# Reordering the fill, the block transitions and the last product of a scan-then-MLP kernel

## The chip, the cores and the metric

The kernel runs on one core of a Trainium2 chip. PE (TensorE) does the matrix products, ACT (ScalarE) and DVE (VectorE) the elementwise work, and SP (SyncE) and POOL (GpSimd) mainly issue DMA transfers. The metric is device time in microseconds (us); a lower one is better. Every time below is a median of the runs of one kernel, with lowest and highest.

## The reference

```python
# batch 4, seq 6144, d_model 256, d_ff 1024
sig = 1/(1 + exp(-f_logit));  f = lb + (1 - lb)*sig;  i = 1 - f
h[t] = f[t]*h[t-1] + i[t]*x[t]          # over the sequence, y[t] = h[t]
out = maximum(y @ w1, y @ w2) @ w_out   # on the 24576 x 256 rows of y
```

## The kernel before

Tokens are handled in 48 blocks of 512. For each block ACT makes the sigmoid ("gate"), DVE makes decay, drive and two scans (one for each half of the channels), PE does the "first layer" (8 groups `fc` of two 512-column matmuls, evicted in pairs by an ACT ReLU), and then the second layer. Blocks 0 to 3 use a plain second layer: 8 pieces of five 256-column matmuls. From block 4 on, two blocks make a pair, and their second layer is a scheme with seven products instead of eight. The input comes in chunks: one block each for the first four, then one pair each, so chunk 4 is blocks 4 and 5. `fT` and `xT` are the transposed `f_logit` and `x` of a chunk, `wd` is the first layer's weight. The instruction order on each engine is the order of the program (`manual_schedule`), so the text below is also the schedule. Lines that the change and the argument touch, with cuts marked:

```python
    nc.vector.tensor_copy(out=ident[:], in_=ident_f[:])
    nc.scalar.activation(out=warm[:], in_=ident_f[:, 0:1], func=AF.Sigmoid)
    nc.vector.tensor_scalar_add(out=nom[:], in0=lbc[:], scalar1=-1.0)   # need lower_bound
    nc.vector.tensor_scalar(out=om[:], in0=lbc[:], scalar1=-1.0, scalar2=1.0, ...)
    fetch_first(0); fetch_first(1)            # ... f_logit and x of block 0, in halves
    ...
    first_bf16(0, 0, nc.vector.tensor_copy)   # casts of the first half
    first_bf16(0, 1, nc.vector.tensor_copy)
    first_turn(0); first_recurrence(0)
    ...
    for fc in range(FC):                      # second layer of block 0
        if fc == 4:
            turn(turn_steps(2)); gate(2)
        second_layer(0, fc)
    ...
    for fc in range(FC):                      # first layer of block 1, alone
        first_layer(1, fc)
    ...
    order = {2: ("decay0", "drive0"), 3: ("scan00",), 4: ("scan01",), ...}   # block 4's, in
    for fc in range(FC):                                                     # block 3's layer
        first_layer(3, fc); second_layer(2, fc)
        if fc in gates: pair_gate(PAIR0, gates[fc])     # gates = {0: 0, 1: 1, 4: 2, 5: 3}
        for t in order.get(fc, ()): scans[PAIR0][t]()
    ...
            for slot in range(2 * FC):        # pair loop
                first_layer(2 * p + slot // FC, slot % FC)
                if first and slot % 2:        # first pair: second layer of block 3
                    second_layer(2 * p - 1, slot // 2)
    # last pair, last product (M4): bank X already holds the sum for another output
    product("X", part(1, 1), given(t4), groups=range(3));           then(leave_last(slice(0, 3)))
    product("Y", part(1, 1), given(t4), True, groups=range(3, 4));  then(leave_last(slice(3, 4)))
```

A group in the fresh bank Y needs what bank X held added later, so ACT takes a snapshot of that group of X before M4 starts. DVE reads bank X first.

Of the kernel before, what the change touches and what calls it, by code (L numbers as in the profile page):

```python
# [18 lines left out]
def kernel(  # L19
# [105 lines left out]
    def first_bf16(k, s, copy):  # L125
        raw = raws[k, s]
        nat = const.tile([P, TB // 2 // P, D], HALF, name=f"nat{k}{s}")
        copy(out=nat[:], in_=raw[:])
        raws[k, s] = nat
# [48 lines left out]
    def turn(steps):  # L178
        for dst, src in steps:
            nc.tensor.transpose(dst, src, ident[:])  # L180
# [276 lines left out]
    def store(j, osb, groups=slice(0, TB // P), cols=slice(0, D), queue=None):  # L457
        b, t0, nb, c, o = blocks[j]
        r0 = b * S + t0
        (queue or nc.sync).dma_start(  # L460
            out=out[r0 : r0 + nb, :].rearrange("(p n) d -> p n d", p=P)[
                :, groups, cols
            ],
            in_=osb[:, groups, cols],
        )
# [58 lines left out]
    def sevenths(p):  # L524

        bank, snap, osbs = {}, {}, {}
        steps = []
        ja, jb = 2 * p, 2 * p + 1
        end = p == NPAIR - 1

        def product(b, left, w, fresh=False, groups=range(TB // P)):
            for i in groups:
                for k in range(KH + 1):
                    new = fresh and i == groups[0] and k == 0
                    steps.append([b, left, w(k), i, k, new, None])

        def then(fn):
            steps[-1][-1] = fn

        def open_bank(b, i=0):  # L540
            if i:
                t = ps_d.tile([P, 2 * TB // P, P], FP32, name="dT")
            else:
                t = ps_o.tile([P, TB // P, P], FP32, name="ps")
            bank[b] = t

        def seed(b, src):
            def go():
                open_bank(b)
                nc.scalar.copy(out=bank[b][:], in_=bank[src][:])  # L550
            return go

        def snapshot(b, name):
            def go():
                t = snpool.tile([P, TB // P, P], FP32, name="sn")
                nc.scalar.copy(out=t[:], in_=bank[b][:])  # L556
                snap[name] = t
            return go

        def leave(b, j, cols, name, last):  # L560
            def go():
                if j not in osbs:
                    osbs[j] = opool.tile([P, TB // P, D], FP32, name="osb")
                dst = osbs[j][:, :, cols]
                if name is None:
                    nc.scalar.copy(out=dst, in_=bank[b][:])  # L566
                else:
                    nc.vector.tensor_tensor(  # L568
                        out=dst, in0=bank[b][:], in1=snap[name][:], op=ALU.add
                    )  # L570
                if end:
                    store(j, osbs[j], cols=cols)
                elif last:
                    store(j, osbs[j])
            return go

        def leave_both(b):
            def go():
                leave(b, jb, hi, 5, False)()
                t = snpool.tile([P, TB // P, P], FP32, name="sn")  # L580
                nc.scalar.copy(out=t[:, 3, :], in_=bank[b][:, 3, :])
                snap[4] = t
            return go

        def leave_last(at):
            def go():
                dst = osbs[jb][:, at, lo]
                if at.start:
                    nc.vector.tensor_tensor(
                        out=dst, in0=bank["Y"][:, at, :], in1=snap[4][:, at, :],  # L590
                        op=ALU.add,
                    )
                else:
                    nc.scalar.copy(out=dst, in_=bank["X"][:, at, :])
                store(jb, osbs[jb], at, lo, nc.sync if at.start else nc.scalar)
            return go

        def sub(n):
            return lambda: sums[p, n]

        def part(t, k2):
            return lambda: rts[2 * p + t, k2]

        def plain(k2, cols):
            a, b = right(k2, cols)
            return lambda k: a[:, k, :] if k < KH else b

        def given(t):
            return lambda k: t[:, k, :]

        product("X", part(0, 0), plain(0, lo), True)
        then(seed("B", "X"))
        product("E", sub(1), given(t1), True)
        then(snapshot("E", 5))
        if end:
            product("B", part(0, 1), plain(1, lo), groups=range(1))
            product("X", sub(2), given(t2))
            then(snapshot("X", 2))
            product("B", part(0, 1), plain(1, lo), groups=range(1, 4))
            then(leave("B", ja, lo, None, False))  # L620
            product("X", sub(3), given(t3))
            then(leave_both("X"))
            product("E", sub(4), plain(1, hi))
            then(leave("E", ja, hi, 2, True))
            product("X", part(1, 1), given(t4), groups=range(3))
            then(leave_last(slice(0, 3)))
            product("Y", part(1, 1), given(t4), True, groups=range(3, 4))
            then(leave_last(slice(3, 4)))
        else:
            product("X", sub(2), given(t2))  # L630
            then(snapshot("X", 2))
            product("B", part(0, 1), plain(1, lo))
            then(leave("B", ja, lo, None, False))
            product("X", sub(3), given(t3))
            then(leave("X", jb, hi, 5, False))
            product("E", sub(4), plain(1, hi))
            then(leave("E", ja, hi, 2, True))
            product("X", part(1, 1), given(t4))
            then(leave("X", jb, lo, None, True))

        def runner(step):
            b, left, w, i, k, fresh, after = step

            def run():
                if fresh:
                    open_bank(b, i)
                a = left()
                cols = slice(i * P, (i + 1) * P) if k < KH else slice(i, TB, TB // P)
                nc.tensor.matmul(  # L649
                    bank[b][:, i, :],  # L650
                    lhsT=a[:, k, cols],
                    rhs=w,
                    start=fresh,
                    stop=after is not None,
                    skip_group_check=True,
                )
                if after is not None:
                    after()
            return run

        return [runner(s) for s in steps]

    with tc.manual_schedule():
        nc.scalar.dma_start(out=lbc[:], in_=lower_bound.rearrange("(h p) -> p h", p=P))
        nc.vector.tensor_copy(out=ident[:], in_=ident_f[:])
        nc.scalar.activation(out=warm[:], in_=ident_f[:, 0:1], func=AF.Sigmoid)
        nc.vector.tensor_scalar_add(out=nom[:], in0=lbc[:], scalar1=-1.0)
        nc.vector.tensor_scalar(
            out=om[:], in0=lbc[:], scalar1=-1.0, scalar2=1.0, op0=ALU.mult, op1=ALU.add
        )  # L670
        fetch_first(0)
        fetch_first(1)
        for g in range(NG):
# [11 lines left out]
            nc.tensor.transpose(wt[:, 0, 0:P], ident[:], ident[:])  # L685
        first_bf16(0, 0, nc.vector.tensor_copy)
        first_bf16(0, 1, nc.vector.tensor_copy)
        first_turn(0)
        first_recurrence(0)
        first_bf16(1, 0, nc.scalar.copy)  # L690
# [30 lines left out]
        for fc in range(FC):  # L721
            if fc == 4:
                turn(turn_steps(2))
                gate(2)
            second_layer(0, fc)
        for step in scan_steps(2):
            step()
        for step in make_sevens():
            step()
        for fc in range(FC):  # L730
            first_layer(1, fc)
        turn(turn_steps(3))
        gate(3)
        early = scan_steps(3)
# [21 lines left out]
                scans[PAIR0][t]()  # L756

        queue, due = [], 0
        for p in range(PAIR0, NPAIR):
            first = p == PAIR0  # L760
            more = p + 1 < NPAIR
# [23 lines left out]
            gates = {4: 0, 6: 1, 12: 2, 14: 3} if more else {}  # L785
            for slot in range(2 * FC):
                first_layer(2 * p + slot // FC, slot % FC)
                if first and slot % 2:
                    second_layer(2 * p - 1, slot // 2)
                if p > PAIR0 + 1 or (p == PAIR0 + 1 and slot >= LAG):  # L790
                    due += NSEV / (2 * FC)
                    while due >= 1:
                        due -= 1
                        queue.pop(0)()
                if slot == 2 and p + 3 < NPAIR:
                    cross(blocks[2 * p + 6][3])
                if slot in gates:
                    pair_gate(p + 1, gates[slot])
                while seq and seq[0][0] < (slot + 1) * 9:
                    seq.pop(0)[1]()  # L800
# [38 lines left out]
```

## Time and profile before

380.15 us (380.11 to 380.67, three runs); the profiled execution spans 378.5 us. From the page of the kernel before, the busy line and the chain of waits:

```profile
PE 367.7 (97%) x4136; PEld 279.2 (74%) x4136; DVE 338.4 (89%) x409; ACT 302.4 (80%) x410; POOL 36.2 (10%) x79
...
PE 92%; DVE 5%; DMA 1%; ACT 0%; issue 0%; DVEq 0%
```

PE is the bound: only time in which PE cannot issue can be won. From the first weights on, the starts of successive matmuls are 216, 109 and 56 ns apart (512, 256 and 128 columns) except at a few places, and each place has an owner.

The fill. From the timeline of the kernel before (start us, busy us, engine, line, operation, tiles, in brackets the idle time before and who ended it), DVE:

```profile
4.63 0.17 DVE L667 TENSOR_SCALAR nom<-lbc 128x2 f32<-128x2 f32 x1 [3.06 <-DMA lbc<-in_lower_bound_dram]
4.71 0.16 DVE L668 TENSOR_SCALAR om<-lbc 128x2 f32<-128x2 f32 x1
4.78 0.42 DVE L128 CAST nat<-osb 128x512 f16<-128x512 f32 x1
...
6.53 0.48 DVE L213 TENSOR_SCALAR ff<-u,nom 128x256 f16<-128x256 f16 x2 [0.72 <-ACT u L258]
6.93 0.68 DVE L223 TENSOR_TENSOR v<-u,ps 128x512 f16<-128x512 f16 x1
```

The cast of f_logit waits behind two tiny operations that wait for lower_bound (complete at 4.61 us); f_logit itself is complete at 4.28 us. The decay (6.53) and the drive (6.93) follow, and the first `wd` matmul comes at 11.75 us.

Blocks 0 to 1. The timeline, PE and then ACT:

```profile
23.97 1.89 PE L441 MATMUL dT<-r,wd 128*128 128x512 f16 x8
26.11 1.94 PE L441 MATMUL dT<-r,wd 128*128 128x512 f16 x8 [0.25 <-ACT r L449]
...
25.04 1.94 ACT L449 ACTIVATE r<-dT 128x1024 f16<-128x1024 f32 x2 [0.28 <-PE dT L441]
```

With nothing between the groups, PE outruns the evictions of its two banks. By the spacing of the starts it loses 0.41 us here (the bracket's 0.25 is shorter because the end of a pipelined matmul is modelled), and 0.05 us a little later.

Into block 4. The timeline, ACT and DVE; the landing of chunk 4's f_logit after its transposing DMA, at 38.12 us, starts this chain:

```profile
38.23 0.63 ACT L285 ACTIVATE u<-fT 128x512 f16<-128x512 f16 x1 [0.95 <-DMA fT<-scr]
38.77 1.00 ACT L449 ACTIVATE r<-dT 128x1024 f16<-128x1024 f32 x1
39.67 0.62 ACT L285 ACTIVATE u<-fT 128x512 f16<-128x512 f16 x1
...
40.32 0.35 DVE L213 TENSOR_SCALAR ff<-u,nom 128x512 f16<-128x512 f16 x1 [1.07 <-ACT u L285]
40.59 0.69 DVE L223 TENSOR_TENSOR v<-u,xT 128x1024 f16<-128x1024 f16 x1
41.19 0.69 DVE L496 COPY osb<-ps 128x512 f32<-128x512 f32 x1
41.79 2.45 DVE L230 TENSOR_TENSOR_SCAN r<-ff,r,v 128x512 f16<-128x512 f16 x2
```

Gate, eviction, gate, decay, drive, copy, two scans follow each other without a gap and end at 44.25 us. Block 4's first layer began at 44.42 us; only its second matmul (44.64 us) needs the second scan. So there was no wait yet, and little room.

Into block 7. The timeline, DVE and then PE:

```profile
50.26 0.69 DVE L496 COPY osb<-ps 128x512 f32<-128x512 f32 x1 [1.81 <-PE ps L487]
...
57.00 0.69 DVE L496 COPY osb<-ps 128x512 f32<-128x512 f32 x1
57.60 1.48 DVE L506 TENSOR_TENSOR S<-r 128x2560 f16<-128x2560 f16 x1
...
60.40 2.46 DVE L230 TENSOR_TENSOR_SCAN r<-ff,r,v 128x512 f16<-128x512 f16 x2
...
58.91 0.22 PE L649 MATMUL ps<-w,r 128*128 128x128 f16 x1
59.14 0.51 PE L649 MATMUL ps<-t,S 128*128 128x128 f16 x6
...
62.23 0.38 PE L441 MATMUL dT<-r,wd 128*128 128x512 f16 x1
62.91 0.38 PE L441 MATMUL dT<-r,wd 128*128 128x512 f16 x1 [0.30 <-DVE r L230]
```

DVE sits idle 1.81 us for a copy of block 3's output and then works without pause to the scan that PE waits for; PE loses 0.46 us. On the way it loses another 0.17 us: its product at 59.14 us needs the sum `S` that DVE makes right after the second copy (57.60 to 59.08).

The end. The timeline, ACT and then PE:

```profile
372.29 0.27 ACT L581 COPY sn<-ps 128x128 f32<-128x128 f32 x1 [1.27 <-DVE osb L568]
...
372.37 0.22 PE L649 MATMUL ps<-w,S 128*128 128x128 f16 x1
372.61 1.00 PE L649 MATMUL ps<-t,r 128*128 128x128 f16 x15
```

M4 starts 0.24 us after the last matmul before it, once ACT's snapshot has left bank X.

### The profile page before, as it was taken

To read this page: it belongs to the slowest core of one execution; us is meant where nothing else is said; L and a number is where in the kernel's file an instruction comes from. 1 tells how busy PE (TensorE), PEld (TensorE's weight loads), DVE (VectorE), ACT (ScalarE), POOL (GpSimd) and SP (SyncE) were. 2 spreads that over 40 slices of the span, in tenths; PEclk is the share of its full clock that TensorE was granted. 3 is DMA by queue.
4 is the path that set the end of the run, shared out by engine and by line. 5 is a ranking of instruction groups with operands and counts; after the bars stand their busy time and mean duration, and the time that the engine had idled before them with its cause. 6 is when DMAs were issued, how large, how long until landed. Compare 5 with 4: busy or idle time off the path is not lost.

```text
span 378.5 us, 9591 instructions
## 1 busy us (share of the span) xinstructions
PE 367.7 (97%) x4136; PEld 279.2 (74%) x4136; DVE 338.4 (89%) x409; ACT 302.4 (80%) x410; POOL 36.2 (10%) x79
## 2 busy tenths in 40 slices
PE   4999999999999999999999999999999999999995
PEld 3677767777777777777777777777777777777784
DVE  4796789999999999999999999999999999999762
ACT  5856788888798798888888887987988888889752
POOL 2500203101101101101001101101101101000000
PEclk9999999999999999999999999999999999999999
DMA  7996999999999989989999999999999999940223
GB/s 248 249 225 130 285 145 222 168 187 258 221 185 264 214 175 283 186 164 266 169 236 263 220 205 301 196 197 276 209 192 270 211 174 188 236 196 4 112 113 113
DMA packets 104797, 77.17 MB, mean 204 GB/s; under 512 B 93554, under 2 KB 95602, under 8 KB 104050
## 3 DMA queue, kind: packets, MB, share of 16 engines
q1 hardware_dynamic: 101538, 51.19, 59.9%
q0 software_dynamic: 2544, 25.17, 33.8%
q8 instruction: 32, 0.52, 0.6%
q10 hardware_dynamic: 672, 0.20, 0.2%
q14 instruction: 11, 0.09, 0.1%
HBM read 53.48 MB, written 48.23 MB: 269 GB/s over the span
## 4 chain that ended last, share of the span: by engine, by line
PE 92%; DVE 5%; DMA 1%; ACT 0%; issue 0%; DVEq 0%
PE ps L649 45%; PE dT L441 42%; PE ps L487 4%; DVE r L230 1%; DVE S L506 1%; DMA lbc<-in_lower_bound_dram 1%; PE ps L180 1%; DVE v L223 1%; DVE r L264 1%; DVE ff L213 0%; PE ps L397 0%; DVE osb L496 0%; ACT r L449 0%; PE ps L137 0%; ACT u L258 0%
## 5 line engine op out<-in xcount | busy, mean ns | idle before, releaser
L449 ACT ACTIVATE r<-dT 128x1024 f16<-128x1024 f32 x192 | 196.0, 1023 | 52.6 <-PE dT L441 52.5
L441 PE MATMUL dT<-r,wd 128*128 128x512 f16 x768 | 225.3, 379 | 1.1 <-DVE wd L365 0.5
L649 PEld LDWEIGHTS <-S 128*128 128x128 f16 x1760 | 115.4, 101 | 37.8 <-issue 0.6
L649 PEld LDWEIGHTS <-r 128*128 128x128 f16 x1320 | 90.9, 101 | 36.7
L230 DVE TENSOR_TENSOR_SCAN r<-ff,r,v 128x512 f16<-128x512 f16 x88 | 108.2, 1271 | 0.8
L649 PE MATMUL ps<-t,S 128*128 128x128 f16 x1320 | 101.6, 219 | 0.0
L506 DVE TENSOR_TENSOR S<-r 128x2560 f16<-128x2560 f16 x44 | 65.4, 1487 | 14.4 <-ACT r L449 14.3
L441 PEld LDWEIGHTS <-wd 128*128 128x128 f16 x768 | 67.6, 113 | 6.4 <-DVE wd L365 1.6
L649 PE MATMUL ps<-wob,r 128*128 128x128 f16 x704 | 69.9, 219 | 0.0
L506 DVE TENSOR_TENSOR S<-r,S 128x2560 f16<-128x2560 f16 x44 | 65.0, 1478 | 0.0
L285 ACT ACTIVATE u<-fT 128x512 f16<-128x512 f16 x88 | 56.1, 637 | 0.9 <-DMA fT<-scr 0.9
L213 DVE TENSOR_SCALAR ff<-u,nom 128x512 f16<-128x512 f16 (+1 forms) x98 | 31.5, 346 | 8.3 <-ACT u L207 3.5
L649 PE MATMUL ps<-w,r 128*128 128x128 f16 x176 | 38.5, 219 | 0.0
L348 POOL CAST waited<-fT 128x1 f32<-128x1 f16 x21 | 9.4, 449 | 280.6 <-DMA fT<-scr 280.6
L649 PE MATMUL ps<-t,r 128*128 128x128 f16 x435 | 34.4, 219 | 0.0
L568 DVE TENSOR_TENSOR osb<-ps,sn 128x512 f32<-128x512 f32 x44 | 30.1, 685 | 3.2 <-PE ps L649 3.2
L649 PE MATMUL ps<-wob,S 128*128 128x128 f16 x352 | 32.6, 219 | 0.0
L223 DVE TENSOR_TENSOR v<-u,xT 128x1024 f16<-128x1024 f16 x44 | 30.2, 686 | 0.0
L556 ACT COPY sn<-ps 128x512 f32<-128x512 f32 x44 | 25.9, 588 | 2.6 <-PE ps L649 2.4
L566 ACT COPY osb<-ps 128x512 f32<-128x512 f32 x43 | 25.1, 583 | 0.8 <-PE ps L649 0.8
L487 PEld LDWEIGHTS <-r 128*128 128x128 f16 x160 | 16.0, 101 | 6.2
L649 PE MATMUL ps<-w,S 128*128 128x128 f16 x88 | 19.3, 219 | 0.0
(58 smaller groups left out, 129.9 us busy)
## 6 DMA issues: line engine op xcount, KB each, us to landing
out_dram<-osb SPq DMA_DIRECT2D x46, 512.0 KB, 4.0
scr<-in_f_logit_dram POOLq DMA_DIRECT2D x22, 512.0 KB, 7.5
scr<-in_x_dram POOLq DMA_DIRECT2D x22, 512.0 KB, 10.4
r<-in_moe_w_dram SPq DMA_DIRECT2D x4, 512.0 KB, 6.9
fT<-in_f_logit_dram POOLq DMA_DIRECT2D x3, 256.0 KB, 7.6
xT<-in_x_dram POOLq DMA_DIRECT2D x3, 256.0 KB, 8.3
out_dram<-osb SPq DMA_DIRECT2D x3, 256.0 KB, 2.6
osb<-in_f_logit_dram SPq DMA_DIRECT2D x2, 256.0 KB, 4.5
```

Of the source, the lines that this page charges most:

```text
L213: nc.vector.tensor_scalar(out=ff[:, h, cols], in0=u[:, h, cols], scalar1=nom[:, h : h + 1], scalar2=1.0, op0=ALU.mult, op1=ALU.add,)
L223: nc.vector.tensor_tensor(out=like(v[:, :, cols], xT), in0=like(u[:, :, cols], xT), in1=xT, op=ALU.mult,)
L230: nc.vector.tensor_tensor_scan(out=y_of(j, h), data0=ff[:, h, o : o + TB], data1=v[:, h, o : o + TB], initial=0.0 if t0 == 0 else y_of(j - ...
L285: nc.scalar.activation(out=mids[p + NBLK, "u"][:, h, cols], in_=held[c, 0][:, h, cols], func=AF.Sigmoid, scale=-1.0,)
L441: nc.tensor.matmul(dT[:, fc % 2, :], lhsT=wd[:, kc, unit_cols(fc)], rhs=y_of(j, kc), start=(kc == 0), stop=(kc == KC - 1),)
L449: nc.scalar.activation(out=rts[j, k][:, g - 1 : g + 1, :].rearrange("p q (i m) -> p q i m", m=P), in_=dT[:].rearrange("p q (m i) -> p q i ...
L487: nc.tensor.matmul(ps[:, r, :], lhsT=left, rhs=right, start=(s == 0 and r == 0), stop=(s == n - 1 and r == 1), skip_group_check=True,)
L506: nc.vector.tensor_tensor(out=t[:], in0=a, in1=b, op=op)
L556: nc.scalar.copy(out=t[:], in_=bank[b][:])
L566: nc.scalar.copy(out=dst, in_=bank[b][:])
L568: nc.vector.tensor_tensor(out=dst, in0=bank[b][:], in1=snap[name][:], op=ALU.add)
L649: nc.tensor.matmul(bank[b][:, i, :], lhsT=a[:, k, cols], rhs=w, start=fresh, stop=after is not None, skip_group_check=True,)
```

## The change

Four parts. *Casts*: the two small operations go behind the first casts. *Block 0*: its last second-layer pieces go among the first-layer groups of block 1. *Block 3*: its pieces reach further into pair 2, and the last into pair 3, so that DVE's copies come later. *M4*: three banks, so that the last evictions are smaller. The diff, cut to its core:

```diff
-        nc.vector.tensor_scalar_add(out=nom[:], ...)          # casts
-        nc.vector.tensor_scalar(out=om[:], ...)
...
         first_bf16(0, 1, nc.vector.tensor_copy)
+        nc.vector.tensor_scalar_add(out=nom[:], ...)
+        nc.vector.tensor_scalar(out=om[:], ...)
...
-            second_layer(0, fc)                               # block 0
+            if fc == 6:
+                first_layer(1, 0)
+                first_layer(1, 1)
+            if fc < 7:
+                second_layer(0, fc)
...
-        for fc in range(FC):
+        for fc in range(2, FC):
             first_layer(1, fc)
+            if fc == 3:
+                second_layer(0, 7)
...
+        pieces3, piece = (1, 3, 5, 9, 11, 13, 15), 0          # block 3
...
-                if first and slot % 2:
-                    second_layer(2 * p - 1, slot // 2)
+                if first and slot in pieces3 or p == PAIR0 + 1 and slot == 1:
+                    second_layer(2 * PAIR0 - 1, piece)
+                    piece += 1
...
-                nc.scalar.copy(out=t[:, 3, :], in_=bank[b][:, 3, :])       # M4
+                nc.scalar.copy(out=t[:, 2:4, :], in_=bank[b][:, 2:4, :])
...
-                store(jb, osbs[jb], at, lo, nc.sync if at.start else nc.scalar)
+                store(jb, osbs[jb], at, lo, nc.sync if at.start == 2 else nc.scalar)
...
-            product("X", part(1, 1), given(t4), groups=range(3))
-            then(leave_last(slice(0, 3)))
-            product("Y", part(1, 1), given(t4), True, groups=range(3, 4))
-            then(leave_last(slice(3, 4)))
+            product("X", part(1, 1), given(t4), groups=range(2))
+            then(leave_last(slice(0, 2)))
+            for i in (2, 3):
+                product("Y", part(1, 1), given(t4), True, groups=range(i, i + 1))
+                then(leave_last(slice(i, i + 1)))
```

More of the change, by code (lines that the diff above doesn't have):

```diff
@@ L666 @@
         nc.scalar.activation(out=warm[:], in_=ident_f[:, 0:1], func=AF.Sigmoid)
-        nc.vector.tensor_scalar_add(out=nom[:], in0=lbc[:], scalar1=-1.0)
-        nc.vector.tensor_scalar(
-            out=om[:], in0=lbc[:], scalar1=-1.0, scalar2=1.0, op0=ALU.mult, op1=ALU.add
-        )
         fetch_first(0)
@@ L687 @@
         first_bf16(0, 1, nc.vector.tensor_copy)
+        nc.vector.tensor_scalar_add(out=nom[:], in0=lbc[:], scalar1=-1.0)
+        nc.vector.tensor_scalar(
+            out=om[:], in0=lbc[:], scalar1=-1.0, scalar2=1.0, op0=ALU.mult, op1=ALU.add
+        )
         first_turn(0)
```

## The prediction

> **What bounds it now.** The page of the kernel before gives PE 97% busy, DVE 89%, ACT 80%, and the chain of waits is 92% PE. In the timeline, from 11.75 us on, PE issues matmuls at their own spacing (216, 109 and 56 ns for 512, 256 and 128 columns) except at few places: about 0.45 us at 24 to 28 us (first layer of block 1 alone, four 0.97 us ACT evictions against 0.87 us of matmuls each), 0.46 us at 62.2 us (second matmul of block 7 waits for the DVE scan), 0.17 us at 58.9, and 0.18 us each at 366.6 and 372.4. The rest is fill and drain. Only tenths can be won.
>
> **Casts.** The first f_logit tile lands at 4.28 us, lower_bound at 4.61; the cast started at 4.78; it can start near 4.32: 0.4 us off the DVE chain that ends at the first weights (11.2 us). Later landings, checked up to 24 us, leave room for it.
>
> **Block 0 into block 1.** Two second-layer pieces (0.55 us each) among the first layer's groups cover the eviction-bound gap: 0.45 us.
>
> **But both meet one wait.** PE would reach block 4's first layer (44.42 us) about 0.8 us early. Its second matmul needs a scan that ends at 44.25; that chain (gate, eviction, gate, decay, drive, copy, two scans) runs back without slack to the landing of fT of chunk 4 at 38.12 us. DMA slices are 90% or more from the weights on, and this change moves no transfer before it. The second matmul ran at 44.64 and can run at about 44.30. So of 0.85 us only about 0.34 survive; either part alone gives nearly that.
>
> **Block 3 into block 4 and pair 3.** Before, DVE sat idle 1.8 us and then did the copy at 50.26 before pair 3's decay. Now the copy comes between the scans, and the last piece comes in pair 3's slot 1. decay0 then waits for ACT's gate (about 49.5) instead. The second copy can now wait for PE until about 56.4 (it was at 57.00), so the DVE chain to the scan that ended at 62.86 gets 0.55 us shorter. PE still stalls about 0.25 us there; its total lead after it is 0.55 us. From there to 366 us I see no wait that would eat it.
>
> **Tail.** The Trainium skill (PSUM — Partial Sum Buffer, on bank collisions) says that no two of PE, ACT and DVE may access one bank (in the same quadrant) at the same time; the trace agrees: PE resumed 0.05 us after ACT's 128x128 copy of bank X. That copy becomes 128x256: from 0.27 us (128 columns) and 0.48 us (384), an estimate of 0.37, so M4 starts 0.10 us later. The smaller last evictions win it back: last landing 376.92 before, 376.88 now without the lead.
>
> **Sum.** 0.55 + 0.04, about 0.6 us: 379.55 us, 379.0 to 380.0. Faster by over 2%: 0.00; within 2%: 0.99; slower: 0.01.
>
> **Signs.** First cast near 4.3 us and weights wd 0.4 us earlier; no PE gap at 25 to 27 us; a new PE wait of some 0.4 us at block 4's first layer on the DVE scan, with fT still landing near 38.1; the wait at block 7 halved; the 128x256 snapshot, and M4 0.1 us later relative to it.
>
> **What would make it wrong.** fT landing earlier or later; steady-state waits that appear when PE leads; two last stores colliding in the ACT queue.

## The result, and the profile after

379.62 us (379.48 to 380.26, four runs), against 380.22 us (380.11 to 380.67, four runs) of the kernel before: 0.60 us less. The ratio of the fast runs is 0.9985, with a 95% interval of 0.9968 to 1.0003. Such a ratio is the mean time of one kernel's fast runs over that of the other's of the same rounds, so it is not quite the ratio of the medians. The interval contains 1, and so does that of a second submission (full2, below): the times alone do not prove a gain, and the traces have to show it. The profiled execution spans 377.7 us, 0.8 us less. From the page of the changed kernel:

```profile
PE 367.9 (97%) x4136; PEld 279.8 (74%) x4136; DVE 338.7 (90%) x410; ACT 302.4 (80%) x410; POOL 35.6 (9%) x79
...
PE 94%; DVE 3%; DMA 1%; issue 0%; SPq 0%; ACT 0%; DVEq 0%
```

The chain of waits now runs through DVE for 3% of the span instead of 5%. The fill, in the timeline of the changed kernel:

```profile
4.22 0.43 DVE L128 CAST nat<-osb 128x512 f16<-128x512 f32 x1 [2.66 <-DMA osb<-in_f_logit_dram]
5.53 0.43 DVE L128 CAST nat<-osb 128x512 f16<-128x512 f32 x1 [0.88 <-DMA osb<-in_x_dram]
5.87 0.16 DVE L685 TENSOR_SCALAR nom<-lbc 128x2 f32<-128x2 f32 x1
...
6.15 0.48 DVE L213 TENSOR_SCALAR ff<-u,nom 128x256 f16<-128x256 f16 x2
6.66 0.69 DVE L223 TENSOR_TENSOR v<-u,ps 128x512 f16<-128x512 f16 x1
```

The first cast came 0.56 us earlier. But the drive needs x as well, which landed at 5.51 us here (5.36 before) and then goes through a cast and PE's transposes: in no trace of this case does the drive start less than 1.15 us after that landing. So it started at 6.66 us instead of 6.93, and the first wd matmul, 4.82 us later in both traces, at 11.48 us instead of 11.75. The small operations, now behind the *second* cast, held the decay until 6.15 us (its gate was done at 5.95), but that cost nothing: with 0.40 us from decay to drive, as before, the drive could have started at 6.55.

Blocks 0 to 1, the timeline, PE:

```profile
22.62 1.03 PE L441 MATMUL dT<-r,wd 128*128 128x512 f16 x4
...
24.03 1.03 PE L441 MATMUL dT<-r,wd 128*128 128x512 f16 x4
...
25.44 1.89 PE L441 MATMUL dT<-r,wd 128*128 128x512 f16 x8
27.17 0.61 PE L180 MATMUL ps<-ident,fT 128*128 128x128 f16 x8
```

No wait is left. Into block 4, the timeline, ACT and then PE:

```profile
37.89 0.63 ACT L285 ACTIVATE u<-fT 128x512 f16<-128x512 f16 x1 [1.33 <-DMA fT<-scr]
...
43.70 1.06 PE L441 MATMUL dT<-r,wd 128*128 128x512 f16 x4
```

The group of four at 43.70 us takes 1.06 instead of 1.03 us: by the starts, its second matmul was 0.04 us late. The gate began 0.34 us earlier than before, because the landing was at 37.78 us and not at 38.12. Into block 7, the timeline, DVE and then PE:

```profile
51.41 0.67 DVE L496 COPY osb<-ps 128x512 f32<-128x512 f32 x1
...
56.08 0.69 DVE L496 COPY osb<-ps 128x512 f32<-128x512 f32 x1 [0.30 <-PE ps L487]
56.68 1.48 DVE L506 TENSOR_TENSOR S<-r 128x2560 f16<-128x2560 f16 x1
...
58.29 0.50 PE L650 MATMUL ps<-t,S 128*128 128x128 f16 x6
...
61.99 0.38 PE L441 MATMUL dT<-r,wd 128*128 128x512 f16 x1 [0.24 <-DVE r L230]
```

The first copy no longer holds anything up, the second now waits 0.30 us for PE, and PE still loses 0.41 us at block 7 (0.46 before; the prediction had it halved). What went is mostly the other wait: the sum is done at 58.16 us, before PE asks for it at 58.29. The end, the timeline, ACT and then PE:

```profile
371.37 0.37 ACT L581 COPY sn<-ps 128x256 f32<-128x256 f32 x1 [1.27 <-DVE osb L568]
...
371.44 0.22 PE L650 MATMUL ps<-w,S 128*128 128x128 f16 x1
371.79 0.72 PE L650 MATMUL ps<-t,r 128*128 128x128 f16 x10
```

The snapshot is 0.10 us longer, and M4 starts 0.35 us after the matmul before it instead of 0.24.

To compare traces, I cut each at the starts of six matmuls. Lengths in us, worked out from the traces:

| segment | predicted change | before | after | change |
|---|---|---|---|---|
| start to the first wd matmul | -0.40 | 11.75 | 11.48 | -0.27 |
| to block 2's first layer | -0.45 | 17.03 | 16.58 | -0.45 |
| to block 4's second matmul | +0.51 | 15.86 | 15.90 | +0.04 |
| to block 7's second matmul | -0.21 | 18.27 | 18.03 | -0.24 |
| to M4 | +0.10 | 309.70 | 309.80 | +0.10 |
| M4 to the end | -0.14 | 5.89 | 5.90 | +0.01 |
| sum | -0.59 | 378.50 | 377.69 | -0.81 |

Five lines are as predicted within 0.15 us, and one, the wait at block 4, is 0.47 us off.

### The profile page after: what moved, and what is told of

The parts are those of the page before. It is cut to its first block, busy times and chain, and to the rows that moved or that the text cites. A ratio compares the mean times of both kernels' runs of the same rounds, so it can differ in the third digit from the quotient of the medians.

```text
span 377.7 us, 9593 instructions
## 1 busy us (share of the span) xinstructions
PE 367.9 (97%) x4136; PEld 279.8 (74%) x4136; DVE 338.7 (90%) x410; ACT 302.4 (80%) x410; POOL 35.6 (9%) x79
## 4 chain that ended last, share of the span: by engine, by line
PE 94%; DVE 3%; DMA 1%; issue 0%; SPq 0%; ACT 0%; DVEq 0%
PE ps L650 44%; PE dT L441 43%; PE ps L487 5%; DMA osb<-in_x_dram 1%; DVE S L506 1%; PE ps L180 1%; DVE r L230 1%; DVE r L264 1%; PE ps L397 0%; DVE v L223 0%; DVE osb L568 0%; DVE osb L496 0%; PE ps L137 0%; DVE osb L589 0%; PE ps L383 0%
```

## The experiments

Twelve runs, all with correct results. The first four share a chip and 11 runs of the kernel before, the next four 9, the last four 11. Segments of all of them (us, "landing" is fT of chunk 4, "wait" is by how much block 4's second matmul comes late, counted from block 2; with the two delays 2.25 of 2.60 and all of 1.60 us arise at block 3):

| kernel | first wd | to block 2 | landing | wait at block 4 | block 4 to 7 | last product to M4 | M4 to end |
|---|---|---|---|---|---|---|---|
| before | 11.75 | 17.03 | 38.12 | 0 | 18.27 | 0.24 | 5.89 |
| after | 11.48 | 16.58 | 37.78 | 0.04 | 18.03 | 0.35 | 5.90 |
| a_casts | 11.19 | 17.03 | 37.85 | 0 | 18.26 | 0.24 | 5.89 |
| c_block0 | 11.53 | 16.57 | 37.28 | 0 | 18.27 | 0.24 | 5.89 |
| ac | 11.26 | 16.61 | 37.65 | 0.10 | 18.26 | 0.24 | 5.89 |
| d_block3 | 11.57 | 17.76 | 38.64 | 0 | 18.03 | 0.24 | 5.92 |
| b_m4 | 11.60 | 17.04 | 37.72 | 0 | 18.27 | 0.35 | 5.90 |
| ac_late | 11.19 | 16.57 | 37.37 | 0 | 18.27 | 0.24 | 5.89 |
| full_act | 11.26 | 16.67 | 37.83 | 0.21 | 17.63 | 0.35 | 5.90 |
| best | 11.61 | 16.83 | 37.62 | 0 | 17.63 | 0.06 | 5.91 |
| full2 | 11.24 | 16.57 | 37.76 | 0.27 | 18.03 | 0.35 | 5.89 |
| full_delay | 11.14 | 16.57 | 39.99 | 2.60 | 18.03 | 0.35 | 5.89 |
| full_delay_late | 11.33 | 16.55 | 39.52 | 1.60 | 18.04 | 0.35 | 5.90 |
| best2 | 11.38 | 16.51 | 37.29 | 0 | 17.63 | 0.06 | 5.89 |

### a_casts: the casts alone

The first part of the diff, nothing else.

> Only the casts part. Fixed-landing theory (fT of chunk 4 lands at about 38.1 us whatever the start does): first wd and block 0's first layer 0.3 to 0.4 us earlier; block 4's second first-layer matmul at about 44.3 instead of 44.64 with a small wait; time 0.3 us less than before. Moving-landing rival (the landing comes earlier when the start does, as in the changed kernel's trace, 37.78): landing near 37.8, no wait at block 4, time 0.3 us less. The landing tells them apart, the time does not.

379.75 us (379.64 to 379.99, five runs), against 380.65 (380.03 to 381.21, 11 runs): ratio 0.9979 (0.9967 to 0.9991). The landing was at 37.85 us, and block 4 did not wait. The first wd matmul came at 11.19 us: the lead of 0.56 us over the first trace went unchanged through every later segment. Part of it is luck: x landed at 5.21 us here, and the drive started 1.15 us after it. Over all traces, the first wd matmul came at 11.61 us on average in the four without the casts (11.53 to 11.75) and at 11.31 in the ten with them (11.14 to 11.61). The casts are worth about 0.30 us.

### c_block0: block 0 alone

The second part of the diff, nothing else.

> Only block 0's second layer reaching into block 1. Both theories: no gap at 25 to 27 us (0.41 us before), and as nothing starts earlier, fT of chunk 4 at about 38.1. Fixed-landing: PE would be 0.46 us ahead at block 4, its second matmul waits about 0.12 us for the scan, lead 0.34 us; time 0.3 us less. Chance rival (the landing just varies by 0.3 us from run to run): landing anywhere from 37.7 to 38.2.

379.79 us (379.46 to 380.64, six runs), ratio 0.9983 (0.9970 to 0.9997). The segment to block 2 is 0.46 us shorter, as the gaps of 0.41 and 0.05 us are gone. The landing was the earliest of all, 37.28 us, although nothing that the landing waits for was moved; this is outside the range that the chance theory had named, too. So a landing before 38.1 us needs no earlier start: that speaks against the moving-landing rival as the explanation, and for chance. With that landing block 4 had no wait.

### ac: casts and block 0 together

> Casts and block 0. Fixed-landing: landing 38.1, PE waits 0.4 us at block 4, time only 0.34 us less than before, no more than either part alone. Moving-landing: landing 37.8, wait under 0.1 us, lead 0.7 us after block 4 and 0.7 us off the time.

379.68 us (379.44 to 379.86, five runs), ratio 0.9975 (0.9963 to 0.9987). The landing was 37.65 us, the wait 0.10 us, and the lead over the first trace 0.83 us at block 7. Neither the 0.34 us nor the 0.4 us wait of the fixed-landing theory came; the numbers of the moving-landing theory nearly did, but c_block0 had such a landing without an earlier start. The rule behind the fixed-landing theory did hold: the second matmul came at 43.82 us, 6.17 us after the landing. It is 6.17 or 6.18 us after the landing in every trace with the copy before the scans in which it waits (after, ac, full_act, full2, full_delay), and later than that where PE itself was later (before 6.51, a_casts 6.23, c_block0 6.68, d_block3 6.54, b_m4 6.78). The times of the three kernels do not tell whether the parts add up, as the kernel before fell into two groups in this batch.

### d_block3: block 3 alone

The third part of the diff, nothing else.

> Only block 3's second layer reaching into block 4 and pair 3. Nothing changes before 44.4 us; landing 38.1 in all theories but chance. DVE's copy of block 3 comes between the scans, the wait of block 7's second first-layer matmul (0.46 us before) falls to 0.1 to 0.25 us: time 0.2 to 0.35 us less.

379.99 us (379.75 to 381.00, five runs), ratio 0.9984 (0.9971 to 0.9997). The segment from block 4 to block 7 is 0.24 us shorter, exactly what it is in the changed kernel. The wait at block 7 missed its range: it is 0.40 us, not 0.1 to 0.25 (the reason is given below). The profiled execution was the slowest of the five and shows how a run can lose 0.7 us: w_out landed at 16.08 us instead of 14.55 (before), and PE waited for it. From the waits between 10 and 20 us of this run (engine, line, who ended it: us in total, times, longest):

```profile
POOL scr L100 <- DMA wob<-in_moe_w_out_dram: 2.9, 1, 2.9
...
PE ps L397 <- DMA wob<-in_moe_w_out_dram: 0.2, 1, 0.2
```

The fetches queued behind it came later too, and fT of chunk 4 landed at 38.64 us. PE lost another 0.39 us at 129.53 us, in no other trace: an addition of DVE had waited 1.0 us for an earlier output to be stored. That the slower group of the other runs has the same cause is not shown; only one execution of each kernel is traced.

### b_m4: M4 in three banks alone

The fourth part of the diff, nothing else.

> Only M4 in three banks. The snapshot becomes 128x256 and takes 0.37 us instead of 0.27, PE's gap before M4 grows from 0.18 to 0.28 us; the last landing, counted from the last product's first matmul or from the product before it, is the same within 0.1 us. Time the same within 0.1 us.

380.84 us (380.09 to 381.01, five runs) against 380.31 (380.14 to 381.04, 9 runs): ratio 1.0005 (0.9993 to 1.0018); three runs fell in the slower group. In the trace the gap before M4 grew from 0.24 to 0.35 us, and from M4 to the end it took 5.90 us as against 5.89. This part costs 0.1 us and wins nothing.

### ac_late: the scans before the copy

```diff
-            2: ("decay0", "drive0"),
-            3: ("scan00",),
-            4: ("scan01",),
+            2: ("decay0", "drive0", "scan00", "scan01"),
```

> Casts and block 0 with both scans of block 4 put before DVE's copy of block 2's first half (0.6 us off the chain from the landing of fT to block 4). If that chain is what clips casts and block 0 together (0.45 us in the times instead of the 0.8 us that the two parts give apart), this gives 0.2 to 0.4 us more than casts and block 0 alone, and no PE wait at block 4 whatever the landing. Rival: the parts are subadditive only by the scatter of the times, and the copy's place changes nothing.

379.54 us (379.29 to 379.83, five runs), ratio 0.9977 (0.9964 to 0.9989). No wait at block 4, but the landing was 37.37 us: with the copy first the scan would have let PE go at 37.37 + 6.17 = 43.54 us, and PE came at 43.62. So this trace tells nothing about the copy, and the ratio is no better than that of ac. Inconclusive; full_delay_late settles it.

### full_act: a copy moved from DVE to ACT

```diff
-                (nc.scalar.copy if j == 0 else nc.vector.tensor_copy)(
+                (nc.scalar.copy if j == 0 or (j, g) == (3, 1) else nc.vector.tensor_copy)(
```

> The whole change, with the copy of block 3's second half moved from DVE to ACT, which was idle 0.83 us there. If the rest of block 7's wait is that copy (0.60 us, and 0.30 us that it waits for PE) in front of two sums and two scans, PE's 0.40 us wait at block 7 goes and the time falls by 0.3 to 0.4 us against the whole change. If PE meets another wait there, less.

379.17 us (379.01 to 379.34, five runs), ratio 0.9967 (0.9955 to 0.9980). Block 4 to block 7 takes 17.63 us instead of 18.03: the wait of 0.41 us is gone, and no other came in its place. So what was left of block 7's wait was this copy on DVE.

### best: a better version

The whole change, the two edits above, and M4 in two banks with the fresh one first:

```diff
-            product("X", part(1, 1), given(t4), groups=range(2))
-            then(leave_last(slice(0, 2)))
-            for i in (2, 3):
-                product("Y", part(1, 1), given(t4), True, groups=range(i, i + 1))
-                then(leave_last(slice(i, i + 1)))
+            product("Y", part(1, 1), given(t4), True, groups=range(2, 4))
+            then(leave_last(slice(2, 4)))
+            product("X", part(1, 1), given(t4), groups=range(2))
+            then(leave_last(slice(0, 2)))
```

> The whole change, with the scans before the copy, the copy on ACT, and M4 in two banks with the fresh bank (groups 2 and 3) first, so that PE need not wait for the snapshot (0.29 us). Expected: no PE wait at blocks 4 and 7 and none before M4; time 0.6 to 0.9 us less than the whole change, about 378.8 us.

378.65 us (378.39 to 379.13, five runs), ratio 0.9952 (0.9938 to 0.9965). The waits at blocks 4 and 7 and before M4 are gone. At block 4 this is not shown to come from the scans' place: with the landings of this trace and of best2 (37.62 and 37.29 us), 6.17 us more would have been early enough in any case. The profiled execution was the slowest of the five. It began slowly: between the start of its first wd matmul and block 2 it took 16.83 us, not 16.57, and the starts of its first three wd matmuls are 427 ns apart, where 216 is the spacing later. The Trainium skill (TensorE: Matmul & The Clock Gate, Part 1) says that an array that was idle runs at half its clock, 426.7 ns for 512 columns; the trace agrees with the number. Here that rate lasted until 12.8 us (the transposes before are 107 ns apart, 56 at the full rate); in best2, the same kernel, it ended at about 11.5 us. So part of this run's length is chance.

### full2: the changed kernel again

> The changed kernel once more, with more rounds, on the chip of the next three runs. Time 379.5 to 379.7 us, 0.6 us less than before. fT of chunk 4 lands between 37.3 and 38.6 us as in the ten traces so far; the wait at block 4's second matmul is near zero for a landing under 37.8 and about the landing minus 37.75 above that.

379.70 us (379.44 to 380.50, six runs) against 380.19 (380.01 to 381.61, 11 runs): ratio 0.9987 (0.9973 to 1.0002). The landing was 37.76 us and the wait 0.27 us, more than the expectation said for that landing: this run's start was 0.24 us quicker than that of the first, so PE came earlier and met the same scan. Its block 4 matmul came at 43.94 us, the first run's at 43.96. That is the clip at work: the quicker start was lost entirely.

### full_delay: one more transfer ahead of chunk 4

```diff
         for c in range(1, 6):
+            if c == 4:
+                nc.gpsimd.dma_start(out=spare[:], in_=srcs[0][0, 0:TB, :].rearrange(...))
```

> The whole change with one more 512 KB input read in the queue ahead of chunk 4 (about 1.25 us of that queue, by the spacing of its landings), into a tile that nothing reads. If the chain from the landing of fT of chunk 4 bounds block 4, fT lands near 39.0, block 4's second matmul is at landing plus 6.15 us, about 45.1 instead of 43.96, and nearly all of that stays in the time: 0.8 to 1.2 us more than the whole change. Rival (that landing has slack, and the leads went elsewhere): under 0.3 us more.

381.28 us (381.15 to 381.67, four runs), 1.58 us more than full2 in the same rounds. In the trace the landing came at 39.99 us, 2.23 us later than in full2 and not 1.25 (the extra read took 1.21 us of the queue as expected, but the last fetch of chunk 5 took 3.66 us instead of 2.46, and the transposes are issued after it), block 4's second matmul at 46.16, and the end 2.23 us later. So the size of the delay was misjudged and the rule held: 39.99 + 6.17 = 46.16. From the timeline, ACT and then PE:

```profile
40.10 0.63 ACT L285 ACTIVATE u<-fT 128x512 f16<-128x512 f16 x1 [3.89 <-DMA fT<-scr]
...
41.69 0.59 PE L442 MATMUL dT<-r,wd 128*128 128x512 f16 x2 [2.09 <-ACT r L450]
...
46.16 0.81 PE L442 MATMUL dT<-r,wd 128*128 128x512 f16 x3 [0.19 <-DVE r L230]
```

Most of the wait now shows one block earlier, at block 3: the eviction of its first groups stands behind the gate in ACT's queue. A late landing holds PE at two places.

### full_delay_late: the same, scans before the copy

The edits of full_delay and ac_late together, on the whole change.

> The same with the scans of block 4 before DVE's copy. The chain from the landing is 0.6 us shorter, but the first eviction of block 3, behind the gate that waits for the landing, holds PE as well (its third pair of groups about 1.9 us late, as four slots of 0.98 us follow to block 4): block 4's second matmul at about 44.8, so only 0.3 us less than with the copy first.

380.86 us (380.61 to 381.03, four runs), 0.42 us less than full_delay in the same rounds. Landing 39.52 us, block 4's second matmul at 45.34: 5.82 us after the landing instead of 6.17. So the copy stood in the chain; taking it out wins 0.35 us of its 0.60, because block 3's eviction then holds PE, as expected.

### best2: the better version again

> The better version once more, on the same chip as the whole change: 378.5 to 378.9 us, 0.7 to 1.1 us less than the whole change, with a PE gap of 0.18 us at most from 20 us to the end.

378.71 us (378.49 to 379.33, six runs), ratio to the kernel before 0.9959 (0.9945 to 0.9972): 0.99 us less than full2 in the same rounds. From the timeline of its end, ACT and then PE:

```profile
370.75 0.37 ACT L581 COPY sn<-ps 128x256 f32<-128x256 f32 x1 [1.27 <-DVE osb L568]
...
370.83 0.22 PE L649 MATMUL ps<-w,S 128*128 128x128 f16 x1
370.89 0.72 PE L649 MATMUL dT<-t,r 128*128 128x128 f16 x10
371.45 0.72 PE L649 MATMUL ps<-t,r 128*128 128x128 f16 x10
```

PE goes straight on with the fresh bank while ACT reads bank X, and comes back to X when the snapshot is long done. From M4 to the end it still takes 5.89 us, so the whole 0.29 us is won. It is 0.48% and 0.41% faster than the kernel before in its two submissions, and it beats the changed kernel.

## Why the prediction was right or wrong

The prediction was right in its sum (379.55 against 379.62 and, again, 379.70 us) and in most of its terms.

- *Casts, "0.4 us off the DVE chain"*: right in kind, about 0.30 us in size. Two landings set the start, and the prediction took both from one trace. There lower_bound landed 0.33 us after f_logit; in the three other traces without the casts it was 0.16 to 0.19 us, so there was less to win. And the drive is held by x too: with x at 5.51 us, in the first trace after, that was the limit, and the chain of waits indeed names that transfer (it named lower_bound before).
- *Block 0, 0.45 us*: right: 0.45 us in the changed kernel, 0.46 alone.
- *"Both meet one wait", of 0.85 us only 0.34 survive*: the mechanism is right and its size was not. The rule, block 4's second matmul not before the landing plus 6.17 us, held in the five traces in which PE waited with the copy first, with landings from 37.65 to 39.99 us, and delaying the landing on purpose delayed everything. No run contradicts "this change moves no transfer before it"; what failed is to read it as *the landing stays at 38.12 us*. In the eleven other traces without an added transfer the landing lay anywhere from 37.28 to 38.64 us. The first trace was a late one. In the two traces of the whole change the wait was 0.04 and 0.27 us, not 0.51. The reason given, that DMA slices are 90% or more throughout, was too coarse as well: the page's slices of 9.5 us hide pauses, and its fourth slice shows 0.6.
- *Block 3, 0.21 us in that segment, with 0.25 us of wait left*: the gain was 0.23 to 0.24 us in all five traces with this part and the copy on DVE; the wait left was 0.40 to 0.41 us and not 0.25. The prediction had listed the 0.17 us wait at 58.9 us but not asked what becomes of it. Block 7's second matmul comes 5.91 or 5.92 us after the second copy starts in all eleven traces with that copy on DVE; the sum behind the copy, now earlier, no longer stops PE, and PE waits for the same chain at block 7 instead. A lead of PE is not the reason: d_block3 has none and waits as long. The rest of the wait was the second copy, as full_act shows.
- *Tail, M4 0.10 us later, won back by smaller evictions*: the first half is right (0.11 us), the second wrong (0.01 us the other way). The last landing did come sooner after M4, 4.23 us (376.02) instead of 4.31, but the end did not hang on it. The semaphore records of the traces show what it hangs on: after its own last store, SyncE waits for the semaphores of the DMA transfers one by one. In the kernel before it waits first for its own 64 KB (landed at 376.76 us), and ACT's 192 KB, which landed at 376.92, stands last in that list and costs nothing. The program ends 1.73 to 1.77 us after the landing that stands first, in all eight traces with two last stores; in best and best2 the other store landed 0.28 us later still. So the store that was made smaller was not the one that held the end. In the changed kernel ACT's second store stands second in the list, and SyncE waits for its landing. Of the durations, the last stores took 2.77 us from issue to landing with 192 KB and 2.45 with 64 KB before, 2.64 with 128 KB and 2.59 to 2.64 with 64 KB after. The Trainium skill (DMA: Bandwidth & Descriptors, Anatomy of one DMA) gives, for transfers issued by GpSimd, a fixed cost of about 2.0 us and a share by bytes, by which 128 KB more are an estimate of 0.30 us. These stores are issued by SyncE and ACT; the pair before agrees with that share (0.32 us), but with three stores in flight 64 KB took about as long as 128.
- *The sum*: in the pair of traces it was 0.81 us and not 0.59, since the wait at block 4 came out 0.47 us smaller, and the start and the tail 0.28 us worse. In the times it was 0.60 and 0.49 us. Part of the trace's 0.81 is that the first trace of the kernel before began 0.14 us later than the average of those without the casts. So the close match of the sum with the times is partly luck: errors of 0.28 and 0.47 us had opposite signs, and the times scatter by more than the rest.

What stays open: why the landing scatters. The traces narrow it. SyncE issues the transposes 0.4 us after x of chunk 5 has landed in DRAM (32.40 to 33.57 us in the undelayed traces), and fT lands 4.72 to 5.26 us after that x; both parts scatter, and no output store is issued before 41.7 us in any trace. No wait for PE, ACT or DVE shows in that chain. An earlier start may shift it a little (37.64 us on average in the eight undelayed traces with the casts, 37.94 in the four without), but the ranges overlap and the mean of the four hangs on one run with late weights.

## What to carry to other kernels

Time won early survives only up to the next wait whose other side does not move; find that side, and how much it scatters between runs, before adding up gains. When one input of an operation is made to arrive earlier, look at when its other inputs arrive: here x was the next limit. When a wait is removed, ask where PE meets the same chain next. Before shrinking the last store, find out which landing the end really waits for. Where a fresh PSUM bank is used at a hand-over, fill it first, while the old bank is still being read: that won the 0.29 us here.

## What the Trainium skill lacked or had wrong

- No page says how far the landing of queued transfers scatters between runs of one schedule: fT of chunk 4 landed between 37.28 and 38.64 us in 12 traces. It would belong to DMA: Bandwidth & Descriptors.
- DMA: Bandwidth & Descriptors gives its formula for transfers issued by GpSimd; worked out for 64 KB it is an estimate of 2.15 us. The last stores of 64 KB, issued by SyncE and ACT while others ran, took 2.44 to 2.64 us.
- PSUM — Partial Sum Buffer tells that engines may not share a bank, in the same quadrant, at once, but not what keeping them apart costs in a hand-over: two readers of one bank in turn put 0.24 us (128 columns) or 0.35 us (256 columns) between two products where 0.06 us is the spacing without it.
